# Batch 0 of a fused attention and Fourier-mix kernel: negated tables and the subtractions of four folds on GpSimd, two more copies on VectorE, dummies among the last transposes, and a last tile cut into 512 and 256 channels

## The chip, the cores and the metric

One core of a Trainium2 chip. The metric is the device time of one execution, in microseconds (us). Nearly all executions here agree within about 1%. All the runs compared below are in the fast state; one slow run of one experiment is left out, and that is told there. Engines carry the profile's names: PE is TensorE (matmul), PEld its weight loads, DVE is VectorE, ACT ScalarE, POOL GpSimd, SP SyncE. "Lnnn" is a line of the kernel's file; the changed kernel has some lines more, so the same instruction has another number there (the values' L521 is L528, the fold's mix L949 is L961).

## The reference, cut to what matters

```python
q, k, v: (8, 12, 448, 64)      # 8 batches, 12 heads
scores = q @ k.T / 8
attn   = maximum(scores, 0)**2 / 448
x      = (attn @ v) as (8, 448, 768)
mixed  = real(fft(fft(x, axis=1), axis=2))
u      = x + mixed
un     = (u - mean(u)) / sqrt(var(u) + 1e-6)
out    = u + maximum(un @ w_ch1, 0) @ w_ch2      # 768 -> 3072 -> 768
```

## The kernel before: the parts that the change and the argument touch

The kernel issues everything by a schedule of its own. Each piece of work asks for an engine, a duration and what it depends on (`need`), and a small simulation in the program picks the next piece. The order on each engine is therefore fixed when the program is built, and on the chip every engine works through its list in that order. This matters below: an instruction that must wait holds up everything behind it on its engine.

All transfers of q, k, v and the weights are issued from POOL:

```python
def load_w1(hf):
    for m in range(MC):                                  # 6 loads of 384 KB per half
        e = yield need("POOL", 0.85)
        t = wpool.tile([128, FF // 2], BF16, name=f"w1_{m}_{hf}")
        nc.gpsimd.dma_start(out=t, in_=moe_w_ch1[...])
        ...
```

The Fourier transform is done as matmuls against sine and cosine tables made at the start (here without the index arithmetic; `seq` for the rows, `chan` for the channels, and their negatives `nseq` and `chan_neg`):

```python
yield from sine(seq[:, 0], ..., e, -1, halfpi)
yield from sine(seq[:, 1], ..., e)
yield from sine(nseq, f[:, :2 * SX], 2 * SX, e, -1)          # on ACT
for m in range(3):
    ...
    yield from sine(chan[m][:, 0, :], ...)
    yield from sine(chan[m][:, 1, :], ...)
    nc.vector.tensor_scalar(chan_neg[:, m], chan[m][:, :, KH:], -1.0, None, op0=ALU.mult)
```

Batch 0 runs before anything else can, so its latency is exposed. For each group of four heads q and k are transposed on PE, copied out of PSUM to `qkT` by DVE (r = 0) and ACT (r = 1), multiplied to scores (`sc`), passed through relu and square (`sq`), multiplied with v ("values"); the result of every two heads is folded, that is, the first half of its columns plus, and minus, the mirrored second half; each fold is then mixed with the channel tables on PE. Short matmuls on zeros, "dummies", fill gaps to keep PE's clock up.

```python
en, copy = (("DVE", nc.vector.tensor_copy), ("ACT", nc.scalar.copy))[r]     # qkT
...
# fold m of batch b
nc.vector.tensor_tensor(f[:, 0, :], x[:, 0:NS], x[:, XH:XH + NS], op=ALU.add)
nc.vector.tensor_tensor(f[:, 1, :], x[:, 0:NS], x[:, XH:XH + NS], op=ALU.subtract)
...
# the mix of fold m
nc.tensor.matmul(first_pps[i][..., t, c0:c1], lhsT=first_folds[m][:, t, n0:n1], rhs=tab, ...)
```

At the end of batch 0 four tiles of `un` are transposed on PE for the first feed-forward, whose first output is the first `hT`. From there on PE runs feed-forward matmuls with the other batches' attention between them. Each output tile of 128 rows is two halves of 384 channels: 24 matmuls, an add, then one store of 384 KB.

## Time and profile before

| | before |
|---|---|
| median (the 3 runs known when the prediction was made) | 616.02 us (615.21 to 616.64) |
| span of the profiled execution | 614.1 us |
| PE busy | 597.2 us, 97% |
| mean granted PE clock | 0.997 |
| 17th and 18th score matmul pairs of batch 0 start | 28.38 and 29.25 us |
| end of batch 0's sixth values | 40.02 us |
| first `hT` starts | 58.54 us |
| last matmul ends | 610.15 us |

The lines that bound this kernel are shown in the prediction below. One view is added here, because the change is read in it afterwards: what PE waits for in the first 60 us (line that waits, releaser: us in sum, times, the longest).

```profile
PE psS L707 <- ACT unT L729: 1.6, 1, 1.6
PE psS L1116 <- DVE warm L215: 1.3, 1, 1.3
PE psF L419 <- DMA qk<-in_k_dram: 1.0, 1, 1.0
...
```

These are the three longest. In the whole list there is no wait for POOL's work or for a fold: PE never waits for the folds that VectorE makes. The longest wait, at L707, is the one among the last transposes, into which the change puts dummies.

### The profile page before, as it was taken

What the parts mean: (1) busy time and instruction counts of PE and PEld (TensorE: products, weight loads), DVE (VectorE), ACT (ScalarE), POOL (GpSimd) and SP (SyncE); (2) the same over time, 40 slices, a digit from 0 to 9 for tenths busy, and PEclk for the clock granted to TensorE, in tenths of its full rate; (3) what the DMA queues carried; (4) which work ended last, traced back from release to release, by engine and by line L of the source; (5) the groups of instructions that cost most, each with busy time, mean ns of one, the idle gap of its engine ahead of it and who ended that gap; (6) DMA issues with size and microseconds to landing.
All of it is one profiled execution on the core that took longest, in us unless ns stands there. A gap on an engine that the chain in (4) does not pass through costs nothing.

```text
span 614.1 us, 10253 instructions
## 1 busy us (share of the span) xinstructions
PE 597.2 (97%) x4055; PEld 329.1 (54%) x4055; DVE 332.1 (54%) x765; ACT 316.9 (52%) x472; POOL 125.9 (21%) x175
## 2 busy tenths in 40 slices
PE   8998999999999899999999999999999999999997
PEld 6565556544455465555445565555445565554464
DVE  6957676965576669545744468644743447110011
ACT  5965772477555568536763167635772246114300
POOL 9342031411142115211420114210310004000000
PEclk9998999999999999999999999999999999999999
DMA  9999998955938994986474785885462215320021
GB/s 126 205 209 227 204 183 116 214 100 96 153 118 165 194 159 163 159 165 119 157 134 107 145 126 166 157 168 97 145 133 60 86 50 181 101 91 20 0 80 76
DMA packets 125072, 82.22 MB, mean 134 GB/s; under 512 B 76256, under 2 KB 113024, under 8 KB 125024
## 3 DMA queue, kind: packets, MB, share of 16 engines
q0 software_dynamic: 40320, 34.07, 34.6%
q1 hardware_dynamic: 84704, 47.50, 32.5%
q8 instruction: 32, 0.52, 0.4%
q14 instruction: 16, 0.13, 0.1%
HBM read 62.91 MB, written 26.69 MB: 146 GB/s over the span
## 4 chain that ended last, share of the span: by engine, by line
PE 83%; ACT 6%; DVE 4%; DMA 2%; SPq 2%; issue 1%; POOL 0%; DVEq 0%; ACTq 0%; POOLq 0%
PE psF L1078 32%; PE psF L1094 32%; PE psF L521 6%; PE psS L535 6%; ACT sq L555 3%; PE psS L974 2%; DMA o<-ubot 1%; PE psS L824 1%; SPq L915 1%; ACT un L870 1%; DMA qk<-in_k_dram 1%; PE psF L419 1%; DVE stats L856 1%; PE psS L602 1%; ACT hT L1055 1%
## 5 line engine op out<-in xcount | busy, mean ns | idle before, releaser
L1078 PE MATMUL psF<-unT,w 128*128 128x512 bf16 (+1 forms) x1152 | 229.6, 354 | 1.5 <-ACT hT L1055 1.5
L555 ACT ACTIVATE sq<-psS 112x896 bf16<-112x896 f32 x192 | 165.0, 916 | 116.7 <-PE psS L535 116.6
L1094 PE MATMUL psF<-w,hT 128*128 128x384 bf16 x1344 | 224.9, 326 | 0.0
L1094 PEld LDWEIGHTS <-hT 128*128 128x128 bf16 x1344 | 129.2, 98 | 92.3 <-issue 8.8
L1078 PEld LDWEIGHTS <-w 128*128 128x128 bf16 x1152 | 109.6, 98 | 111.9 <-issue 15.8
L1055 ACT ACTIVATE hT<-psF 128x512 bf16<-128x512 f32 (+1 forms) x180 | 98.2, 547 | 98.8 <-PE psF L1078 97.7
L561 DVE TENSOR_TENSOR sq<-sq 112x896 bf16<-112x896 bf16 x192 | 115.8, 619 | 49.9 <-ACT sq L555 48.3
L1063 DVE TENSOR_TENSOR o<-psF,o 128x384 f32<-128x384 f32 x56 | 31.0, 554 | 109.4 <-PE psF L1094 106.8
L442 DVE TENSOR_SCALAR xT<-psF 128x224 bf16<-128x224 f32 x48 | 18.7, 390 | 75.6 <-PE psF L521 75.5
L300 POOL DMA_DIRECT2D vn<-in_v_dram x24 | 17.2, 716 | 177.6 <-PE psF L521 159.3
L535 PE MATMUL psS<-qkT 64*112 64x448 bf16 x384 | 52.4, 367 | 0.9 <-ACT sq L555 0.4
L521 PE MATMUL psF<-sq,vn 112*64 112x448 bf16 x384 | 45.5, 358 | 2.8 <-DVE o L1063 1.8
L844 POOL TENSOR_TENSOR u<-tp,xn 128x385 f32<-128x385 f32 (+1 forms) x14 | 17.3, 1237 | 105.5 <-DVE tp L835 91.6
L535 PEld LDWEIGHTS <-qkT 64*112 64x112 bf16 x384 | 20.4, 125 | 27.8 <-issue 22.5
L870 ACT ACTIVATE un<-u,nmr,rstd 128x768 bf16<-128x768 f32 (+1 forms) x28 | 28.3, 1022 | 7.8 <-DVE nmr L865 7.6
L521 PEld LDWEIGHTS <-vn 112*64 112x64 bf16 x384 | 18.3, 109 | 24.4 <-issue 16.2
L856 DVE BATCH_NORM_STATS2 stats<-u 128x6 f32<-128x384 f32 (+1 forms) x56 | 28.1, 540 | 0.0
L892 POOL DMA_INDIRECT ubot<-u,back x16 | 16.6, 1041 | 39.8 <-DVE hT L1053 26.3
L300 POOL DMA_DIRECT2D qn<-in_q_dram x21 | 15.3, 729 | 23.6 <-DVE sq L561 9.2
L1116 PE MATMUL psS<-warm 128*128 128x126 bf16 (+1 forms) x218 | 18.0, 231 | 1.3 <-DVE warm L215 1.3
L892 POOL DMA_INDIRECT nbot<-un,back x12 | 11.7, 973 | 35.8 <-ACT un L870 32.1
L449 DVE TENSOR_SCALAR xT<-psF 128x224 bf16<-128x224 f32 x47 | 18.1, 384 | 0.0
(117 smaller groups left out, 361.3 us busy)
## 6 DMA issues: line engine op xcount, KB each, us to landing
out_dram<-o SPq DMA_DIRECT2D x28, 384.0 KB, 2.5
vn<-in_v_dram POOLq DMA_DIRECT2D x24, 224.0 KB, 5.3
qn<-in_q_dram POOLq DMA_DIRECT2D x21, 224.0 KB, 6.3
kn<-in_k_dram POOLq DMA_DIRECT2D x21, 224.0 KB, 6.9
w<-in_moe_w_ch_dram POOLq DMA_DIRECT2D x12, 384.0 KB, 13.6
w<-in_moe_w_ch_dram POOLq DMA_DIRECT2D x4, 1152.0 KB, 22.6
utop<-u SPq DMA_DIRECT2D x8, 384.0 KB, 2.6
o<-utop SPq DMA_DIRECT2D x8, 384.0 KB, 3.6
```

The source lines that it names most:

```text
L300: nc.gpsimd.dma_start(out=t, in_=src[b, hs].rearrange("h (p j) d -> p h (j d)", j=4))
L521: nc.tensor.matmul(av[h * Dh:(h + 1) * Dh, 0:S], lhsT=vn[:, c, h0 + h, :], rhs=sq[:, h, :], start=(c == 0), stop=(c == 3))
L535: nc.tensor.matmul(sc[:R, h, 0:S].rearrange("k (c q) -> k c q", c=4), lhsT=kT[ps, m % 2, c, :], rhs=qT[ps, m % 2], start=True, stop=True)
L555: nc.scalar.activation(r, sc[:R, :, 0:S], AF.Relu)
L561: nc.vector.tensor_tensor(r, r, r, op=ALU.mult)
L856: nc.vector.bn_stats(stats[:n, hf, :], u[:n, hf * (D // 2):(hf + 1) * (D // 2)])
L870: nc.scalar.activation(un[:n], u[:n], AF.Identity, bias=nmr[:n, i:i + 1], scale=rstd[:n, i:i + 1])
L892: nc.gpsimd.indirect_dma_start(out=bot, out_offset=bass.IndirectOffsetOnAxis(ap=back[ch][:s1 - s0], axis=0), in_=us[1][:s1 - s0], in_offse ...
L1055: nc.scalar.activation(h[:, 0:N], ph[:, 0:N], AF.Relu)
L1063: nc.vector.tensor_tensor(o[:, hs], pc[:, 0:D // 2], o[:, hs], op=ALU.add)
L1078: nc.tensor.matmul(ph[:, 0:N], lhsT=w1_sb[m][hf][:, jj * 128:(jj + 1) * 128], rhs=unT[:, m, 0:N], start=(m == 0), stop=(m == MC - 1))
L1094: nc.tensor.matmul(pc[:, 0:D // 2], lhsT=hT[j][:, c * 128:(c + 1) * 128], rhs=w2_sb[j // 6][:, j % 6, hs], start=(j == 0), stop=(j == JC - 1))
```

## The change

Its intent is to take work from ACT and DVE, which set the pace of batch 0 in its first half, and give it to POOL, which is 21% busy; and to shorten the tail. Cut to its core:

```diff
-        yield from sine(nseq..., f[:, :2 * SX], 2 * SX, e, -1)
+        e = yield need("POOL", 0.75, [dft_ready])
+        nc.gpsimd.tensor_scalar(nseq, seq[:, 1], -1.0, None, op0=ALU.mult)
...
-            nc.vector.tensor_scalar(chan_neg[:, m], chan[m][:, :, KH:], -1.0, None, op0=ALU.mult)
+            e = yield need("POOL", 0.6, [dft_ready])
+            nc.gpsimd.tensor_scalar(chan_neg[:, m], chan[m][:, :, KH:], -1.0, None, op0=ALU.mult)
...
-            en, copy = (DVE, ACT)[r]
+            en, copy = (DVE, ACT)[r if b > 0 or g == 0 else 0]      # groups 1, 2 of batch 0: DVE
...
     def fold(b, m, F, av, av_end):
+        pool = b == 0 and m < 4
-        nc.vector.tensor_tensor(f[:, 1, :], ..., op=ALU.subtract)
+        if pool:
+            e1 = yield need("POOL", 0.6, [ex + LATENCY["DVE"]])
+        eng = nc.gpsimd if pool else nc.vector
+        eng.tensor_tensor(f[:, 1, :], ..., op=ALU.subtract)
...
             # after the second of the four last transposes
+            for i in range(16 if t == 1 else 0):
+                nc.tensor.matmul(bank[0][:, 384:512], lhsT=warm[:, 0:128], rhs=warm[:, 0:128], ...)
...
-            for half in range(2):                    # 384 and 384 channels, one store per tile
+            cut = 512 if b == B - 1 and c == NC - 1 else D // 2
+            for hs in (slice(0, cut), slice(cut, D)):     # last tile: 512 and 256, a store for each
```

More of the change, by code (lines that the diff above doesn't have):

```diff
@@ L267, in build_dft @@
         yield from sine(seq[:, 1, :, :].rearrange("p a s -> p (a s)"), f[:, :2 * SX], 2 * SX, e)
-        yield from sine(nseq.rearrange("p a s -> p (a s)"), f[:, :2 * SX], 2 * SX, e, -1)
+        e = yield need("POOL", 0.75, [dft_ready])
+        nc.gpsimd.tensor_scalar(nseq, seq[:, 1], -1.0, None, op0=ALU.mult)
         for m in range(3):
@@ L275, in build_dft @@
             yield from sine(chan[m][:, 1, :], y[:, 2 * KH:], 2 * KH, e)
-            e = yield need("DVE", 0.3, [dft_ready])
-            nc.vector.tensor_scalar(chan_neg[:, m], chan[m][:, :, KH:], -1.0, None, op0=ALU.mult)
-            dft_ready.t = e + LATENCY["DVE"]
+            e = yield need("POOL", 0.6, [dft_ready])
+            nc.gpsimd.tensor_scalar(chan_neg[:, m], chan[m][:, :, KH:], -1.0, None, op0=ALU.mult)
+            dft_ready.t = e + LATENCY["POOL"]
     GRP = 4 * R * HG * Dh * 4
@@ L420, in turn_on_pe @@
                                             loads[i][x][:, c, 2 * r + h, :], ident[:R, :R])
-            en, copy = (("DVE", nc.vector.tensor_copy), ("ACT", nc.scalar.copy))[r]
-            e2 = yield need(en, (0.75, act(2 * S))[r], [e1 + LATENCY["PE"]])
+            en, copy = (("DVE", nc.vector.tensor_copy), ("ACT", nc.scalar.copy))[r if b > 0 or g == 0 else 0]
+            e2 = yield need(en, 0.75 if en == "DVE" else act(2 * S), [e1 + LATENCY["PE"]])
             copy(both.rearrange("q x (c r) p -> q r x c p", r=2)[:, r],
@@ L436, in fold @@
     def fold(b, m, F, av, av_end):
-        e1 = yield need("DVE", 2 * dve(HS) + 2 * dve2(NS), [av_end],
+        pool = b == 0 and m < 4
+        e1 = yield need("DVE", 2 * dve(HS) + (1 if pool else 2) * dve2(NS), [av_end],
                         [BX[m]] + ([BA[m]] if m < 3 else []))
@@ L449, in fold @@
             nc.vector.tensor_scalar(xb, ab, 1.0 / (64.0 * S), None, op0=ALU.mult)
-        BF.give(av, e1 - 2 * dve2(NS))
+        ex = e1 - (1 if pool else 2) * dve2(NS)
+        BF.give(av, ex)
         if b > 0:
-            sch.add(turn_x(b, m, e1 - 2 * dve2(NS) + LATENCY["DVE"]), (1, 1))
+            sch.add(turn_x(b, m, ex + LATENCY["DVE"]), (1, 1))
         else:
-            x_ready[b][m].t = e1 + LATENCY["DVE"]
+            x_ready[b][m].t = ex + LATENCY["DVE"]
         f = work.tile([128, 2, NS], BF16, name="fold", bufs=1,
@@ L457, in fold @@
         nc.vector.tensor_tensor(f[:, 0, :], x[:, 0:NS], x[:, XH:XH + NS], op=ALU.add)
-        nc.vector.tensor_tensor(f[:, 1, :], x[:, 0:NS], x[:, XH:XH + NS], op=ALU.subtract)
         F.append(f)
+        if pool:
+            e1 = yield need("POOL", 0.6, [ex + LATENCY["DVE"]])
+        eng = nc.gpsimd if pool else nc.vector
+        eng.tensor_tensor(f[:, 1, :], x[:, 0:NS], x[:, XH:XH + NS], op=ALU.subtract)
         if b == 0:
             first_folds.append(f)
-            f_ready[m].t = e1 + LATENCY["DVE"]
+            f_ready[m].t = e1 + LATENCY["POOL"]
         elif m >= 3:
@@ L711, in turn @@
             done[t] = [e + LATENCY["PE"]] * 2
+            for i in range(16 if t == 1 else 0):
+                nc.tensor.matmul(bank[0][:, 384:512], lhsT=warm[:, 0:128], rhs=warm[:, 0:128], start=True, stop=True)
+            if t == 1:
+                yield need("PE", 16 * 0.055)
         def unload(t, ens):
@@ L1057, in relu, with add @@
             ht[j].t = e + LATENCY["ACT"]
-        def add(pc, e, c, half):
-            hs = slice(half * (D // 2), (half + 1) * (D // 2))
-            e = yield need("DVE", dve(D // 2), [e + LATENCY["PE"], ot[c]])
+        def add(pc, e, c, hs):
+            w = hs.stop - hs.start
+            e = yield need("DVE", dve(w), [e + LATENCY["PE"], ot[c]])
             o = os[c]
-            nc.vector.tensor_tensor(o[:, hs], pc[:, 0:D // 2], o[:, hs], op=ALU.add)
+            nc.vector.tensor_tensor(o[:, hs], pc[:, 0:w], o[:, hs], op=ALU.add)
             BF.give(pc, e)
-            if half == 1:
+            last = b == B - 1 and c == NC - 1
+            if last or hs.stop == D:
                 t0 = T0 + c * 128
                 e = yield need("SP", 0.1, [e + LATENCY["DVE"]])
-                nc.sync.dma_start(out=rows[t0:t0 + 128, :], in_=o)
-                BO.free.append(sch.dma(e, 128 * D * 4))
+                cs = hs if last else slice(0, D)
+                nc.sync.dma_start(out=rows[t0:t0 + 128, cs], in_=o[:, cs])
+                e = sch.dma(e, 128 * D * 4)
+            if hs.stop == D:
+                BO.free.append(e)
                 if c + 2 < NC:
@@ L1085, in ffn @@
         for c in range(NC):
-            for half in range(2):
-                hs = slice(half * (D // 2), (half + 1) * (D // 2))
+            cut = 512 if b == B - 1 and c == NC - 1 else D // 2
+            for hs in (slice(0, cut), slice(cut, D)):
+                w = hs.stop - hs.start
                 for jq in range(4):
-                    e = yield need("PE", 6 * mm(D // 2), ht[6 * jq:6 * jq + 6] + [w2_ready[jq]],
+                    e = yield need("PE", 6 * mm(w), ht[6 * jq:6 * jq + 6] + [w2_ready[jq]],
                                    [BF] if jq == 0 else [])
@@ L1093, in ffn @@
                     for j in range(6 * jq, 6 * jq + 6):
-                        nc.tensor.matmul(pc[:, 0:D // 2], lhsT=hT[j][:, c * 128:(c + 1) * 128],
+                        nc.tensor.matmul(pc[:, 0:w], lhsT=hT[j][:, c * 128:(c + 1) * 128],
                                          rhs=w2_sb[j // 6][:, j % 6, hs],
                                          start=(j == 0), stop=(j == JC - 1))
-                        if c == NC - 1 and half == 1:
+                        if c == NC - 1 and hs.stop == D:
                             BH[j].free.append(e)
-                    advance(6 * mm(D // 2))
-                sch.add(add(pc, e, c, half), (0, 0))
+                    advance(6 * mm(w))
+                sch.add(add(pc, e, c, hs), (0, 0))
     def warming():
```

## The prediction

> **What bounds the kernel now.** I read the page first: the engine table and the chain of work that ended last.
>
> ```profile
> PE 597.2 (97%) x4055; PEld 329.1 (54%) x4055; DVE 332.1 (54%) x765; ACT 316.9 (52%) x472; POOL 125.9 (21%) x175
> ...
> PE 83%; ACT 6%; DVE 4%; DMA 2%; SPq 2%; issue 1%; POOL 0%; DVEq 0%; ACTq 0%; POOLq 0%
> ```
>
> TensorE is busy nearly throughout, and the chain is 83% TensorE. All that the change touches lies at the two ends, so I asked next who TensorE waits for between 60 and 612 us: four kinds of waits, 5.2 us in sum, the longest single one 1.8 us. From about 60 us on, TensorE's own work sets the pace. I also compared the instruction order of the two built programs: from the first feed-forward on, TensorE's matmuls stand in the same order in both, up to the last tile. So the change in time is (a) by how much the first 60 us, batch 0, shift, plus (b) what the last tile saves.
>
> Batch 0: the chain in order of time, cut to the stretch that will decide.
>
> ```profile
> 28.38 0.40 PE psS L535 x2
> 28.77 0.43 PE psS L949 x2
> 29.21 0.11 PE psS L1116 x2
> 29.32 0.33 PE psS L535 x2
> 29.65 0.44 PE psS L1116 x6
> 30.08 0.88 PE psF L521 x8
> ...
> 39.12 0.90 PE psF L521 x8
> 40.02 0.02 issue
> ```
>
> Columns: start, length, what. Before this stretch the chain runs mostly over ScalarE: relu passes over the scores (sq L555, four of them in 3.3 us) and the table sines. From 28.38 to 40.02 us it is TensorE alone, back to back: scores (L535), the channel mix of one fold (L949), warming dummies (L1116), values (L521). The reader should note 28.77: there the third fold is mixed, right behind the seventeenth score.
>
> GpSimd, to which work is moved, in order of time:
>
> ```profile
> 16.22 0.53 POOL L327 DMA_DIRECT2D w<-in_moe_w_ch_dram  x1 [0.61 <-DMA qk<-in_k_dram]
> 17.91 0.53 POOL L327 DMA_DIRECT2D w<-in_moe_w_ch_dram  x1 [1.17 <-DMA vn<-in_v_dram]
> ...
> 22.88 0.53 POOL L327 DMA_DIRECT2D w<-in_moe_w_ch_dram  x1 [0.64 <-DMA kn<-in_k_dram]
> 24.77 0.53 POOL L327 DMA_DIRECT2D w<-in_moe_w_ch_dram  x1 [1.36 <-DMA w<-in_moe_w_ch_dram]
> ...
> 30.34 0.53 POOL L327 DMA_DIRECT2D w<-in_moe_w_ch_dram  x1 [1.29 <-DMA w<-in_moe_w_ch_dram]
> ```
>
> Busy only 0.5 us at a time, it looks free. But each bracket says that the engine stood still in front of a weight load until an older transfer had landed: k, v, then q and k of later groups, then w. Each load waits for the one issued eight before it (the built program says the same), and at 20 to 30 us the transfers run at the 212 GB/s of that stretch, one 384 KB load per 1.85 us. The last of the twelve w1 loads is not issued before 30.34 us. An instruction placed behind it on GpSimd cannot start before about 30.87.
>
> The clock, microsecond by microsecond (the third column from the end is the granted clock, as a share of full speed):
>
> ```profile
> 51.00:52.00 1.00, 0.00 (x0) 0.00 (x0) 0.88 (x3) 1.00 (x3) 0.71 (x1) 1.00 1.11 301
> ...
> 55.00:56.00 1.00, 0.69 (x19) 0.67 (x17) 0.52 (x2) 0.95 (x3) 0.00 (x0) 0.68 1.34 205
> 56.00:57.00 1.00, 1.00 (x13) 0.54 (x9) 1.00 (x3) 0.21 (x1) 0.00 (x0) 0.50 1.24 207
> 57.00:58.00 1.00, 1.00 (x5) 0.45 (x3) 0.88 (x2) 0.00 (x0) 0.00 (x0) 0.50 1.19 215
> 58.00:59.00 1.00, 0.98 (x4) 0.25 (x3) 0.00 (x0) 0.46 (x1) 0.00 (x0) 0.61 1.12 204
> ```
>
> Half speed from within 55 us to within 58 us; the missing shares, (0.32 + 0.50 + 0.50 + 0.39) / 0.5, make 3.4 us at half speed, with TensorE nearly always busy in it: a loss of about 1.6 us. Ahead of it TensorE had idled from 50.9 to 52.6 and again from 53.2 to 54.3.
>
> **What the Trainium skill says.** "TensorE: Matmul & The Clock Gate", section "What's actually happening": the array runs at half rate until it has been busy for a window of 3413 ns, falls back after an idle window, and the window is free-running, so its phase is chance. The trace agrees with the length (3.4 us) and shows that a window need not be empty: if one ended where half speed began, at about 55.7, TensorE had been busy 1.65 us of its 3.41; in the one before, 2.0 us busy, and that one did no harm. "GPSIMD Engine Reference", section "4.1 Engine selection": two-input elementwise work is about twice as slow as on VectorE, one-input work roughly at line rate. The trace agrees in direction: the 112x385 add of u takes 0.905 us on POOL and 0.549 on DVE. The same page, section "1. Specifications", says that GpSimd shares its SBUF interfaces with VectorE's two-input instructions; the 128x385 add, 1.568 us on POOL beside DVE's adds, fits. No page that I found bears on the wait for the eighth transfer back.
>
> **The change part by part.**
>
> Negated tables. The negated sine table leaves ACT: one 480-wide sine, 0.6 us from start to start (8.81 to 9.41). On POOL: a one-input instruction from two rows, 0.25 us at 1 element and 0.98 at 768, so 0.95 ns per element: 0.71 us for 480. It runs at about 9.5 and delays the loads of group 2 by as much; those land at 14.8 or later behind a full queue, so no cost. Three channel negations (0.26 us each) leave DVE and cost 0.62 each on POOL.
>
> Folds. Four 225-wide subtractions (0.19 us start to start) leave DVE. On POOL, from 0.19 us at 1 element and 0.905 at 385: 1.85 ns per element, 0.61 us each.
>
> Copies. Two ACT copies of 0.79 us go to DVE at 0.54. So ACT sheds 0.6 + 1.6 = 2.2 us, and DVE ends even (gains 1.1, sheds 0.8 + 0.8).
>
> What ACT would gain. I replayed the new order by hand with the old durations. The new order asks for group 1's k transposes between the third and fourth scores, and k lands at 5.82 + 6.3 = 12.1 us: ACT loses 0.6 there. ACT's state of 16.84 us (six scores, first sines) comes at 16.4; later the DVE queue, and 22 dummies put after the eleventh score, take part of it back. TensorE gets to the third fold's mix at about 28.3 instead of 28.7. So of the 2.2 us, about 0.4 arrive.
>
> What takes it away. In the changed order on POOL the third channel negation and the third and fourth folds stand behind the twelfth w1 load. That load goes out at 30.34 as before: it still waits for the load eight before it, and the landings are set by bandwidth; issuing some loads 1 to 2 us later leaves the queue full. Then 0.53 (issue) + 0.62 (negation) + 0.61 (fold) + 0.1 (two handovers) = 32.2 us. TensorE executes in order, and the mix of the third fold stands ahead of the eighteenth score: everything waits from 28.3 to 32.2, an idle stretch of 3.9 us. The first two folds are harmless: fold 0 ready at about 18.3 for a mix at 18.4, fold 1 at 24.0 for 23.5 (half a microsecond of waiting, absorbed by the later one).
>
> From there to the end of the sixth values batch 0 was TensorE-bound without gaps: 28.71 to 39.94, 11.2 us. The new order of that stretch has 38 dummies for 30, summed up instruction by instruction 11.5 us, ending at 32.2 + 11.5 = 43.7. Shift: **+3.8 us**.
>
> Clock after the stall. 3.9 us idle exceed a window, so at least one window falls below what already brought half speed in the trace. About 3.3 us of the following TensorE-bound work at half speed: **+1.6 us** (0.9 to 2.5 by phase).
>
> Dummies amid the last transposes. Sixteen 128-wide matmuls of 0.055 us, 0.88 us, inside the idle 1.65 us from 50.9: no cost. They lift the worst window from 0.7 to about 1.55 us busy; 1.65 still brought half speed. I give them half a chance to save the 1.6 us: **-0.8 us**.
>
> Last tile. 24 matmuls of 512 and 24 of 256 stream as many columns as 48 of 384. The last add, 0.56 us at 384, shrinks by 128 / 0.96 = 0.13. The last store shrinks from 384 to 128 KB. It landed 2.3 us after its issue; loads of 96 and 384 KB on that queue landed in 2.0 and 3.1, or 3.8 ns per KB, which makes at most 1.0 for 256 KB; I take 0.55 as an estimate. **-0.7 us**.
>
> Sum: 3.8 + 1.6 - 0.8 - 0.7 = +3.9, on 616.0: **619.9 us**; I shade it to 619.5 for the first rival.
>
> **The rivals.** First: no stall, because POOL gets through its loads sooner or TensorE comes later anyway. Then the ACT relief (1 to 2 us), the clock window (0.8 to 1.6) and the tail (0.7) add up to a gain: 612 to 614. For it: POOL is 21% busy, and the change was evidently built to shift load. Against it: 30.34 in the trace, a queue at full bandwidth, and the order of the program. I give it one in five. Second: the stall occurs without the half-speed window, because scattered work keeps the window busy enough: 618. Third: the stall, half speed twice (after it, and again at the last transposes as now): 622. Fourth: POOL's folds are slowed to 1.0 us each by VectorE; while TensorE stands, VectorE has nothing to do, so this adds at most 0.5.
>
> **Range and chances.** With the stall 617.5 to 622.5, without it 612 to 614.5; eight in ten is 614.0 to 622.5. 2% is 12.3 us, beyond every path here: faster 0.01, same 0.97, slower 0.02.
>
> **What would show it.** Right: TensorE idle in front of the third fold's mix (L961 of the changed kernel) for 3 to 4 us, released by POOL's fold (L466), which follows a w1 load issued at 30 to 31 us; PEclk at a half in the slice after; first relu (hT) later by 4 to 5 us; the last store 128 KB, span end nearer to the last matmul by 0.7. Wrong: the third fold on POOL before 29 us, no wait on L466 over 1 us, or ACT busy without a break up to 35 us.

## The result, and the profile after

| | before | changed |
|---|---|---|
| median (4 runs each) | 615.62 us (615.07 to 616.64) | 620.86 us (620.37 to 623.02) |
| span of the profiled execution | 614.1 us | 618.4 us |
| mean granted PE clock there | 0.997 | 0.992 |
| 17th and 18th score pairs start | 28.38, 29.25 | 32.4, 36.32 |
| end of the sixth values | 40.02 | 48.14 |
| first `hT` starts | 58.54 | 65.32 |
| last matmul ends | 610.15 | 615.16 |

The changed kernel is 0.9% slower: the ratio is 1.009, with a 95% interval of 1.0061 to 1.0119. A ratio here is the mean time of one kernel's fast runs over that of the other's in the same rounds, so it is not quite the ratio of the medians quoted.

The last four rows subtracted: PE is 4.0 us late at the 17th score pair, 7.1 at the 18th, 8.1 at the end of the sixth values, 6.8 at the first feed-forward, 5.0 at the last matmul, and the span is 4.3 longer. So the loss is all made in the first 50 us, and nearly half of it is given back.

What PE waits for in the first 60 us of the changed kernel, the view shown above of the kernel before:

```profile
PE psS L961 <- POOL fold L466: 2.5, 2, 2.1
PE psF L420 <- DMA qk<-in_k_dram: 2.2, 1, 2.2
...
PE psF L420 <- DMA qk<-in_q_dram: 1.0, 1, 1.0
...
```

The first line is the wait that the prediction named. The other two are waits for q and k of the second group of heads, 3.2 us in sum. The kernel before has no such wait: its 1.0 us for k, up to 7.7 us, is for the first group.

POOL in order of time, the view that the prediction shows of the kernel before (start, length, what; in the bracket the idle time ahead of it and what ended it):

```profile
10.45 1.46 POOL L269 TENSOR_SCALAR nseq<-seqm 128x480 bf16<-128x480 bf16 x1
11.86 0.79 POOL L301 DMA_DIRECT2D qk<-in_q_dram  x1
...
31.04 0.53 POOL L328 DMA_DIRECT2D w<-in_moe_w_ch_dram  x1 [1.29 <-DMA w<-in_moe_w_ch_dram]
32.86 0.53 POOL L328 DMA_DIRECT2D w<-in_moe_w_ch_dram  x1 [1.29 <-DMA w<-in_moe_w_ch_dram]
33.41 1.20 POOL L278 TENSOR_SCALAR channeg<-chan 128x386 bf16<-128x386 bf16 x1
34.58 0.61 POOL L466 TENSOR_TENSOR fold<-xT 128x225 bf16<-128x225 bf16 x1
```

Read it from the bottom. The third fold takes 0.61 us, but it stands behind a channel negation, and that stands behind the twelfth w1 load. The two loads shown last each stood 1.29 us until an earlier w1 load had landed. The negation and the fold wait with them, although neither has anything to do with w1. At the top: negating `seq` took 1.46 us, and the loads of the third group went out at 11.86 instead of 9.53.

The chain of work that ended last goes through the same place. Here is the piece of it that answers to the chain from 28.38 us shown of the kernel before, where it was PE back to back:

```profile
22.50 10.08 DMA w<-in_moe_w_ch_dram
32.58 0.28 issue
32.86 0.05 POOL w L328
32.91 0.50 issue
33.41 1.20 POOL channeg L278
34.62 0.58 POOL fold L466
35.20 0.05 issue
35.25 0.51 PE psS L961
```

A weight load issued at 22.50, ten microseconds in flight, now sets when batch 0 goes on.

The clock, microsecond by microsecond (columns: stretch, span, then busy PE, PEld, DVE, ACT, POOL with counts, then the granted PE clock, the DMA share and GB/s). First the wait for k, then the wait for the fold:

```profile
12.00:13.00 1.00, 0.00 (x0) 0.00 (x0) 0.06 (x1) 0.29 (x1) 1.00 (x2) 1.00 0.40 47
13.00:14.00 1.00, 0.14 (x6) 0.14 (x8) 0.00 (x0) 0.00 (x0) 1.00 (x2) 1.00 0.61 40
14.00:15.00 1.00, 1.00 (x16) 0.53 (x14) 0.71 (x2) 0.39 (x1) 1.00 (x3) 0.77 1.39 186
...
33.00:34.00 1.00, 0.20 (x1) 0.00 (x0) 0.60 (x2) 1.00 (x2) 0.98 (x2) 1.00 1.06 209
34.00:35.00 1.00, 0.00 (x0) 0.00 (x0) 1.00 (x2) 0.32 (x1) 1.00 (x2) 1.00 1.12 223
35.00:36.00 1.00, 0.75 (x6) 0.59 (x7) 0.68 (x1) 0.00 (x0) 0.19 (x1) 0.51 1.03 203
```

Both waits are followed by half speed: from 14.5 to 21.4 us and from 35.0 to 38.4, 6.8 and 3.4 us, that is two of the windows of 3.4 us that the prediction speaks of, and one. Note also the last column of the first two lines: at 12 to 14 us the memory traffic falls to 47 and 40 GB/s. The transfers issued by then had nearly drained while POOL was still at its negation and its next issues. Nothing is at half speed from 55 to 66 us any more, where the kernel before had one window.

The tail is as intended: from the last matmul's end to the end of the span it was 614.1 - 610.15 = 3.95 us, and it is 618.4 - 615.16 = 3.24.

### The profile page after: what moved, and what is told of

Read it like the earlier page. It is cut to its first block, busy times and chain, and to the rows that moved or that the text cites. A ratio compares the mean times of both kernels' runs of the same rounds, so it can differ in the third digit from the quotient of the medians.

```text
span 618.4 us, 10279 instructions
## 1 busy us (share of the span) xinstructions
PE 600.5 (97%) x4058; PEld 331.4 (54%) x4077; DVE 333.7 (54%) x760; ACT 315.8 (51%) x469; POOL 134.8 (22%) x183
## 4 chain that ended last, share of the span: by engine, by line
PE 79%; DVE 6%; DMA 5%; ACT 5%; issue 2%; SPq 1%; POOL 1%; DVEq 0%; ACTq 0%; POOLq 0%
PE psF L1112 32%; PE psF L1094 30%; PE psF L528 6%; PE psS L542 6%; PE psS L986 2%; ACT sq L562 2%; DMA w<-in_moe_w_ch_dram 2%; DVE stats L868 1%; DMA qk<-in_k_dram 1%; DMA qkT<-qkr 1%; PE psS L836 1%; ACT un L882 1%; SPq L927 1%; DMA o<-ubot 1%; ACT hT L1067 1%
## 5 line engine op out<-in xcount | busy, mean ns | idle before, releaser
L1094 PE MATMUL psF<-unT,w 128*128 128x384 bf16 (+1 forms) x1134 | 227.5, 352 | 2.2 <-ACT hT L1067 1.1
L1112 PE MATMUL psF<-w,hT 128*128 128x384 bf16 (+2 forms) x1343 | 224.8, 326 | 0.1
L568 DVE TENSOR_TENSOR sq<-sq 112x896 bf16<-112x896 bf16 x192 | 117.4, 627 | 52.9 <-ACT sq L562 51.3
L1075 DVE TENSOR_TENSOR o<-psF,o 128x384 f32<-128x384 f32 (+2 forms) x56 | 31.1, 554 | 107.7 <-PE psF L1112 106.6
L445 DVE TENSOR_SCALAR xT<-psF 128x224 bf16<-128x224 f32 x48 | 18.8, 391 | 78.2 <-PE psF L528 78.1
L882 ACT ACTIVATE un<-u,nmr,rstd 128x768 bf16<-128x768 f32 (+1 forms) x28 | 28.3, 1021 | 7.5 <-DVE nmr L877 7.5
L1134 PE MATMUL psS<-warm 128*128 128x126 bf16 (+1 forms) x224 | 19.8, 243 | 1.3 <-DVE warm L215 1.3
L1134 PEld LDWEIGHTS <-warm 128*128 128x128 bf16 x224 | 15.0, 109 | 6.2 <-issue 4.4
```

The lines of the kernel that those rows point to most:

```text
L568: nc.vector.tensor_tensor(r, r, r, op=ALU.mult)
L882: nc.scalar.activation(un[:n], u[:n], AF.Identity, bias=nmr[:n, i:i + 1], scale=rstd[:n, i:i + 1])
L1075: nc.vector.tensor_tensor(o[:, hs], pc[:, 0:w], o[:, hs], op=ALU.add)
L1094: nc.tensor.matmul(ph[:, 0:N], lhsT=w1_sb[m][hf][:, jj * 128:(jj + 1) * 128], rhs=unT[:, m, 0:N], start=(m == 0), stop=(m == MC - 1))
L1112: nc.tensor.matmul(pc[:, 0:w], lhsT=hT[j][:, c * 128:(c + 1) * 128], rhs=w2_sb[j // 6][:, j % 6, hs], start=(j == 0), stop=(j == JC - 1))
L1134: nc.tensor.matmul(first_pps[0][:, t, c0:512], lhsT=warm[:, 0:128], rhs=warm[:, c0:512], start=not begun, stop=False)
```

## The experiments

Theory A: POOL's queue is the cause. The folds (and the negations) stand behind w1 loads that wait for older transfers, and PE stands behind the folds; the half speed follows from that. Rival B: the folds are harmless, and the loss comes from the early request of q and k (the 3.2 us and the two windows behind it). Rival C: the negated tables cost it, because POOL is slow at them. Rival D: the copies, the dummies or the tail do harm by themselves. Each experiment is a part undone or done alone. Unless said otherwise the short diffs are against the changed kernel. Every run gave correct results.

### 1. Nothing on POOL

The copies, the dummies and the tail are kept; tables and folds stay on ACT and DVE.

```diff
-        nc.gpsimd.tensor_scalar(nseq, ...)              # and chan_neg, and the folds
+        yield from sine(nseq, ...)                      # as in the kernel before
```

> Nothing is moved to GpSimd: negated tables and folds stay where they were; copies, dummies and the narrower last tile are in. Both theories (the third fold waiting behind the weight loads; the k transposes asked for too early since the negated sine left ScalarE) have the cause in what moved to GpSimd, so both expect a time below the kernel before: 0.7 us from the tail, up to 1.6 from the half-speed window that the dummies take away, up to 1.6 from the copies: 612.5 to 614.5 us against 615.6. A time of 618 or more would mean that the copies or the dummies are to blame.

Measured: 612.89 us (7 runs, 610.99 to 613.55) against 615.37 for the kernel before on the same chip (37 runs); ratio 0.9944, interval 0.9924 to 0.9964. Rival D falls: these three parts gain 0.6%. First `hT` came at 56.41 us.

### 2. The folds back on VectorE

All the change but `pool`:

```diff
-        pool = b == 0 and m < 4
+        pool = False
```

(written as the kernel before has it).

> The change without the four folds on GpSimd; the negated tables are there still. Theory A (third fold behind the twelfth weight load decides): no wait on GpSimd's fold, one half-speed window less, 614 to 616 us. Theory B (negated sine on GpSimd: k of group 1 asked for before it lands, group 2's loads issued 2 us later, half speed after the wait at 11.5 to 13.9 us): the delay of some 4 us up to the third fold stays, 618 to 620 us.

Measured: 614.14 us (22 runs, 611.62 to 617.91); ratio 0.9989 (0.9972 to 1.0005). PE doesn't wait for POOL in batch 0 in its trace, only 0.8 us for a fold of VectorE; for q and k it waits 1.1 us in sum, and no half speed follows. Rival B, which had the time stay at that of the changed kernel although the folds are gone, falls as the main cause: up to the first values PE's order is the changed kernel's, so what the early request costs on average is in these 22 runs too. Four subtractions of 0.6 to 0.8 us on POOL, 2.8 us of its work, are worth about 1% of the whole time. Between this run and the one before lie the negated tables: the mean times are 614.44 and 612.76, so they cost about 1.7 us, and they alone aren't the loss of the change. Which part of those 1.7 us is clock stays open.

### 3. The negated tables back, the folds on POOL

```diff
-        nc.gpsimd.tensor_scalar(nseq, ...)              # and chan_neg
+        yield from sine(nseq, ...)                      # chan_neg on DVE
```

> The change without the negated tables on GpSimd; the four folds are there still. The loads go out as in the kernel before, so the third fold is ready at 30.34 + 0.53 + 0.61 = 31.5 us, for a TensorE that gets there at about 28.5. Theory A: a wait of 2.5 to 3.5 us in front of the third fold's mix and a half-speed window behind it, 617.5 to 620 us. Theory B: the early part is cured, and the fold's wait is a small thing: 613 to 616 us.

Measured: 621.91 us (5 runs, 621.66 to 623.96); ratio 1.0099 (1.0073 to 1.0126), worse than I expected. Rival C falls: with no table on POOL at all the loss is as large as in the whole change. PE's waits and POOL's order show why it was more than expected:

```profile
PE psS L960 <- POOL fold L465: 8.4, 2, 6.0
```

```profile
32.03 0.53 POOL L327 DMA_DIRECT2D w<-in_moe_w_ch_dram  x1 [1.29 <-DMA w<-in_moe_w_ch_dram]
32.58 0.63 POOL L465 TENSOR_TENSOR fold<-xT 128x225 bf16<-128x225 bf16 x1
```

In this schedule it is already the second fold that stands behind the twelfth load, and PE waits 6.0 us for it. Which fold is caught depends on the order that the program's schedule gives; that one is caught does not.

### 4. The schedule told that loads wait for the eighth before

The schedule doesn't know that a load stands until the one issued eight before it has landed; it believes that a load costs POOL 0.85 us. Told of it, it puts the third negation and the third fold ahead of the last two w1 loads. No work is moved to another engine.

```diff
+    def eighth(self):
+        return [self.landed[-8]] if len(self.landed) >= 8 else []
...
-            e = yield need("POOL", 0.85)
+            e = yield need("POOL", 0.85, sch.eighth())        # at each load
```

> The whole change, but the scheduler's model is told that a GpSimd load waits for the landing of the eighth before it; the third negation and third fold then stand ahead of the last two w1 loads. In the trace of the change that makes the third fold ready at about 33.5 instead of 35.2 us. Theory A: the 2.05 us wait in front of the third fold's mix shrinks to under 0.5, and the half-speed window behind it is gone: 3 us less than the change, about 617.5 us. Theory B: the early part stays and the rest of the delay returns elsewhere: 619.5 us or more.

Measured: 617.31 us (14 runs, 615.09 to 622.27); ratio 1.0023 (1.0003 to 1.0043). The time is as expected; that no half speed would be left is not. PE's wait for the third fold fell to 0.47 us; the first fold now cost 1.66 us, with two half-speed windows behind it (21 to 27.6 us).

### 5. The second six w1 loads issued only after the fourth fold

The folds stay on POOL, the tables too, and the order on PE is nearly the same; only what they stood behind is taken away.

```diff
     def load_w1(hf):
         for m in range(MC):
-            e = yield need("POOL", 0.85)
+            e = yield need("POOL", 0.85, [f_ready[3]] if hf else [])
```

> The whole change, with one thing taken away: the second six w1 loads are put on GpSimd's queue only after the fourth fold, so that no negation and no fold stands behind a load that waits. TensorE's order in batch 0 stays nearly the change's, negated tables stay on GpSimd. Theory A (folds behind waiting loads): no wait of TensorE on GpSimd's folds over 0.5 us, no half-speed window behind the third fold, 613.5 to 616.5 us, 4.5 to 7 less than the change. Theory B (what the negated tables did to the first 15 us, or that GpSimd is simply slower at this work): 618 us or more, with TensorE still late at the third fold.

Measured: 615.34 us (14 runs, 612.85 to 618.07); ratio 0.9998 (0.9979 to 1.0017), within what was expected. This is the most direct of the tests, for it leaves every piece of POOL work in place. POOL in it, where each fold follows its negation or its data at once:

```profile
27.90 1.40 POOL L278 TENSOR_SCALAR channeg<-chan 128x386 bf16<-128x386 bf16 x1 [3.32 <-ACT chan L254]
29.27 0.97 POOL L466 TENSOR_TENSOR fold<-xT 128x225 bf16<-128x225 bf16 x1
```

PE's waits for folds are 0.9 us in sum, and its trace has no half-speed window in batch 0; the first `hT` came at 59.47 us instead of 65.32. About 5.5 us of the change's time come back. Some 2 of them are clock: the mean granted clock of the 14 executions is 0.997, that of the four of the change 0.993, and a step of 0.003 goes with 1.2 to 1.6 us (experiment 6); this is an estimate. The rest is not clock: PE's waits for folds and for q and k of the second group sum to 1.6 us in this trace and to 5.7 in that of the change. It is still no better than the kernel before and, by the medians, 2.5 us slower than experiment 1 (by the ratios 0.5%): the relief of ACT and DVE that the folds were to bring doesn't arrive.

### 6. The three other parts, each alone

Each is the kernel before with one hunk of the change: the tail, the dummies among the last transposes, the two copies.

> The kernel before with the last tile in 512 and 256 channels alone. From the trace of the change, last matmul to end of span is 3.24 us against 3.95: 0.7 us less, 614.9 against 615.6. Rival: store and add are hidden or the 256-wide matmuls cost more, no gain.

> The kernel before with the sixteen dummies alone. If they keep the clock up between the last transposes: no half-speed window between 50 and 60 us in the trace, and 0.8 us less on average (up to 1.6). If the window falls elsewhere by chance: the half-speed window is there still, and the time is that of before.

> The kernel before with the two copies moved from ScalarE to VectorE alone. ScalarE sheds 1.6 us before the scores end, but TensorE is back to back from 28 us on, so only what brings TensorE there sooner counts: 0.5 to 1.2 us less than before, 614.4 to 615.1. Rival: VectorE, 90% busy until 30 us, becomes the bound, and the time is that of before or worse.

| part alone | median | ratio (95%) |
|---|---|---|
| tail 512 + 256 | 614.65 us (22 runs) | 0.9977 (0.9960 to 0.9995) |
| dummies | 613.80 us (22 runs) | 0.9980 (0.9961 to 1.0000) |
| copies | 613.92 us (21 fast runs of 22) | 0.9971 (0.9954 to 0.9987) |

The kernel before ran 67 times beside them, median 615.42. Multiplied the three ratios give 0.993, and experiment 1 measured the three together as 0.9944: they add up. By the ratios the tail and the copies gain 1.4 and 1.8 us where 0.7 and 0.5 to 1.2 were expected, but the intervals reach down to 0.3 and 0.8; that of the dummies ends at no difference. What the dummies do shows in the clock. With them 14 of 22 executions had a mean granted clock of 0.998 or more; of 104 executions of the kernel before in experiments 1 to 6, 18 had.

Those 104 executions also give an estimate of the price of a half-speed window. Sorted by mean clock their mean times are, for the commonest values and the lowest, 614.03 us at 1.0 (14 runs), 614.97 at 0.996 (20), 615.60 at 0.997 (31), 616.80 at 0.994 (25) and 619.61 at 0.990 (3). The steps from 1.0 to 0.997 and on to 0.994, a window each, go with 1.6 and 1.2 us; the last goes with more, 2.8 us for 0.004, but has three runs. How many windows one execution has varies from run to run of the same program. At an equal clock of 0.994 the changed kernel took 620.84 us (2 runs) and the kernel before, in other batches of runs, 616.80, so about 4 us of the loss are not clock.

### 7. The change again, and with the wait filled

The changed kernel unaltered; and the changed kernel with 40 dummies, 2.2 us, ahead of the matmul that waits for the third fold. They are to keep PE busy through the wait, so that no half speed follows it.

```diff
             for t in range(2):
+                for _ in range(40 if i == 0 and m == 2 and t == 1 else 0):
+                    nc.tensor.matmul(first_pps[0][:, 0, 2 * KH:512], lhsT=warm[:, 0:128], rhs=warm[:, 2 * KH:512], ...)
```

> The changed kernel itself once more, for a number on the chip that the others of this batch run on: 620 to 623 us, and a trace in which the third fold's mix waits 1.5 to 3 us for GpSimd with a half-speed window behind it. If the wait for k at 12 to 14 us is a chance of the one trace, it is under 1 us here; if the early request makes it, it is 1.5 us or more again.

> The whole change, and 40 more dummies (2.2 us at full clock) directly ahead of the matmul that waits for the third fold, so that TensorE works while it would stand; nothing else of its order moves. If the half-speed window behind the wait comes from the idling and is a cost of its own, the window at 35 to 39 us is gone and the time is 1 to 1.7 us under the change's, with the wait for the fold (now hidden behind dummies) still paid. If the window is chance, or only the wait costs, the time is the change's within 0.5 us. If TensorE were not waiting there, the dummies would cost 2.2 us more.

Measured: the change again 619.86 us (6 runs, 618.46 to 622.04), ratio 1.0075 (1.0053 to 1.0096) against 616.08 for the kernel before (11 runs). With the wait filled 622.39 us (6 runs, 619.72 to 625.53), ratio 1.0106 (1.0080 to 1.0132). I expected a gain, and it is slower by 2.2 us in the mean; the intervals overlap, so what is shown is that there is no gain of the size expected. In the trace of the change again PE waited 1.6 us for the third fold.

The dummies did what they were for, PE in order of time:

```profile
32.63 0.34 PE L964 MATMUL psS<-chan,fold 128*128 128x386 bf16 x1
32.81 2.36 PE L959 MATMUL psS<-warm 128*128 128x126 bf16 x40
35.01 0.33 PE L964 MATMUL psS<-chan,fold 128*128 128x386 bf16 x1
```

The second half of the mix starts at 35.01 with no wait in front of it, and no half speed follows. They also did it in the mean: the granted clock of these six executions is 0.9935, of the change again 0.9907, which is the one window less that I expected, though the six values of each scatter by more (0.984 to 0.997, and 0.986 to 0.997). But the time didn't follow; at the same 0.997 the three executions with the wait filled took 619.72 to 622.61 us, and the one of the change again 620.22. Three things in the two traces speak to that. The third fold was ready at 34.61 us, so the dummies held PE 0.4 us longer than it had to wait. The second fold was waited for 1.80 us instead of 0.45, with half speed from 28 to 31.8 us behind it; so the first `hT` came at 64.94 us, no earlier than in the change again (64.73). And from there to the last matmul it took 553.0 us against 549.7, of which 1.7 are one wait at 215 us, of a values matmul for the bank that an output add empties:

```profile
PE psF L528 <- DVE o L1078: 2.0, 1, 2.0
```

In the change again that wait is 0.3 us. Its size is scattered over these kernels' traces with no rule that I found: 1.8 in the kernel before, 2.1 in experiment 1 (a fast kernel), none in experiment 5. The rest of the 3.3 us wasn't traced. So the half speed behind the stall can be had back, but it isn't shown that the time can.

### 8. Experiment 1 with more dummies

Experiment 1 with 12 more dummies behind the third of the last transposes, since what is left in its trace is waits there. The diff is against experiment 1.

```diff
-            for i in range(16 if t == 1 else 0):
+            for i in range((0, 16, 12, 0)[t]):
```

> The version without anything on GpSimd (copies, dummies, narrower last tile, 612.9 us) with twelve more dummies behind the third of the last transposes. If the worst window is still too empty with sixteen: more of the executions at a mean clock of 0.999 or better than the 4 of 7 before, and 612.2 us. If sixteen are enough or the windows lie elsewhere: 612.5 to 613.2, no difference. In either case it stays under both kernels.

Measured: 611.32 us (6 runs, 610.92 to 615.05); ratio 0.9939 (0.9916 to 0.9961); five of six executions were at a clock of 1.0. It is the fastest kernel here and beats both: the kernel before by 0.6%, and the change again, on the same chip, by 1.3%. That it is faster than experiment 1 (ratio 0.9944) is not shown: the intervals overlap.

## Why the prediction was right or wrong

The predicted time, 619.5, is 1.4 us below the 620.86 measured, and the direction and the mechanism held: the third fold stood behind the twelfth w1 load, and PE behind the fold. Experiments 2 and 5 show it from two sides: take the folds from POOL, or the loads from in front of them, and by the medians 6.7 and 5.5 us come back. But several terms of the sum were off, and the total is near because they cancelled.

- *What bounds the kernel: PE from 60 us on, so that the change is the shift of batch 0 plus what the last tile saves.* Held only in part. The loss was made in batch 0, but of the 6.8 us at the first `hT` 1.8 were given back afterwards. 1.4 of them are the one wait of the values for an output add, 1.84 us before and 0.40 after; the other waits from there on sum to 3.4 us before and 3.5 after, so the remaining 0.4 isn't explained. I had counted 5.2 us of such waits and taken them as fixed; part of it is slack that a shift uses up in one trace and not in another (experiment 7).
- *Negated row table: 0.71 us, no cost; the twelfth w1 load "goes out at 30.34 as before", for loads issued later leave "the queue full".* This step failed. The negation took 1.46 us on POOL. Before it, three one-element instructions that make an index took 0.46, 0.52 and 0.52 us instead of 0.25, 0.19 and 0.18; VectorE's table arithmetic began at 8.05 us there and not at 8.65, so that they ran beside it: each ended within 0.1 us after the VectorE instruction next to it. The third group's loads were issued 2.3 us later, and the traffic fell to 40 GB/s at 13 us: the queue ran low. The twelfth load went out at 32.86. The negation is not the whole of that: in experiment 3, without any negation on POOL, the index instructions were as slow, the traffic fell to 131 GB/s at 11 us and to 79 at 15, and the twelfth load went out at 32.03. So of the 2.5 us, 1.7 came without the negations. The slow index instructions are not the change's work: the traces of the dummies alone and of experiment 8, with nothing on POOL, show them too (0.44 to 0.59 us), and that of experiment 5, with the change's tables and folds, doesn't (0.18 to 0.26). In the six traces of kernels with nothing on POOL the twelfth load goes out anywhere from 30.21 to 31.24 us, so up to 0.9 of the 1.7 can be scatter; what the folds among the loads add stays open.
- *Channel negations: 0.62 us each.* 1.20, 1.18 and 1.20 measured. *Folds: 0.61.* 0.83, 0.67, 0.61 and 0.71 measured: right, apart from the first.
- *Waiting for k: 0.6 us.* 3.2 us for q and k, with two half-speed windows behind. The early request for the second group's transposes I had seen in the new order, but k landed at 13.8 us, not at 12.1. In the change again it landed at 12.2 and q at 11.0; PE waited 1.8 us for q, and three half-speed windows lay up to 21 us. In experiments 2, 4, 5 and the filled wait of 7, whose kernels start alike, the waits were 0.9, 1.2, 0.7 and 1.2 us and no half speed lay there up to 20 us. So the early request costs a wait in every one of these traces, of a size that varies, and half speed with it in two of six: a term missing from the sum, and its half speed one of chance.
- *Stall of 3.9 us at the third fold.* 2.05, plus 0.43 at the second. Both its ends moved: the fold was ready at 35.2 and not 32.2, and PE was there at 32.9 and not 28.3, for it had lost 4.0 us at q and k and at half speed already. The sum of the two, PE going on at 35.25, is 3.1 us later than predicted.
- *Shift at the end of the sixth values: 3.8 + 1.6 = 5.4 us.* 8.1 measured: 4.0 up to the 17th score pair, 3.1 between it and the 18th (the wait, the first of the half speed), 1.0 after that (the rest of the half speed). That the stall is followed by one window of half speed, 3.4 us long, was right.
- *The window before half speed in the kernel before.* It was misread a little. By the prediction's own shares half speed began at 55.4 us and not at 55.7; the 3.41 us up to there held 1.68 us of PE's work, and the 3.41 before those held 2.38, not 2.0. What follows from it, that such a window need not be empty, stands.
- *Dummies among the last transposes: half a chance to save 1.6 us.* Right in kind: the window at 55 to 59 us is gone, and 1.3 us of the shift are made good between the sixth values and the first `hT`. Alone they gain 0.2%, in median 1.6 us, with an interval that ends at no difference.
- *Last tile: -0.7 us.* 3.95 to 3.24, so -0.71. The last add took 0.42 us for 0.56, and the last store landed 1.7 us after its issue instead of 2.3.
- *Rivals.* "No stall" at 612 to 614 is what the change without POOL's work does (experiment 1, 612.89). "Half speed twice", 622, came closest in kind: it was three windows, two of them before the stall.

What stays open: which part of the negated tables' 1.7 us is clock, why experiment 5 remains some 2.5 us behind experiment 1 (its trace has a new wait of 1.2 us of PE for a piece of `un` that POOL makes, which isn't all of it), and where the kernel with the filled wait lost the rest of its time.

## What to carry to other kernels

An engine that issues transfers is not idle when its busy share is low: where each load waits for an older one to land, everything placed behind it in the same queue waits as well. Before moving compute there, read from the trace when the queue's last waiting load goes out, and place the compute, or the loads, so that nothing on the critical path stands behind one. And measure an instruction on its new engine with its own type and size before giving its cost as nothing: here each negation took twice its estimate, in the same queue.

## What the Trainium skill lacked or had wrong

- "GPSIMD Engine Reference", section "4.1 Engine selection", calls one-input work on GpSimd roughly line-rate. The negation of a bf16 table took 1.46 us for 480 elements per partition and 1.20 for 386, against 0.26 us for the latter on VectorE. One-input work that I had used as a measure, of another type, took 0.98 us for 768. The page gives no rate by type.
- No page that I found says that a load issued on GpSimd can stand until the one issued eight before it has landed, as the loads of this program do: 1.29 us ahead of each of the last two w1 loads. The compute behind them stands with them, 6.0 us of waiting on PE in experiment 3.
- "TensorE: Matmul & The Clock Gate", section "What's actually happening", lets the clock fall after an idle window of about 3.4 us. Waits of 2.05 and 2.2 us were enough here, with one and two windows of half speed behind them; in the 3.41 us ahead of half speed PE had been busy for 1.58 and 1.21 us, and for 1.68 in the kernel before, so the window need not be idle. By the mean clocks a window goes with 1.2 to 1.6 us in this kernel, and their number varies between executions of the same program.
